# Transposed layernorm tiles of one chunk tracked in separate buffers instead of one

## The chip, the cores and the metric

One core of a Trainium2 chip. The metric is device time in microseconds (us) of one execution. "The granted clock" is the share of TensorE's full clock that the records show, as a mean over the run, rounded: 1.000 leaves room for about 1.2 us at half clock, 0.999 for 1.2 to 3.5 us (worked out from the rounding and a span of 1164 us).

## The reference, cut to what matters

The program is one transformer block with adaptive layernorm: 2048 tokens, width 1024, 32 query heads on 4 key/value heads with 512 cached positions, then a SwiGLU network of width 3584.

```python
h = _layernorm(x) * (1 + ca) + sa
x = x + ga * _A_ref(h, A_k_cache, A_v_cache, A_wq, A_wo)     # attention, output projection
h = _layernorm(x) * (1 + cb) + sb
x = x + gb * _B_ref(h, B_w_gate, B_w_up, B_w_down)           # gate, up, down
```

`h` is the moving operand of matmuls. The kernel keeps it for them as `hT`, with its width on the partitions, so it transposes the normalized tile.

## The kernel before

The tokens are worked on in chunks of 512 (four tiles of 128). Seven of the eight chunk layernorms of the program are made as follows (the very first one goes through TensorE). VectorE normalizes a tile into one of two buffers `nsc`, SyncE issues a DMA transpose of it into a quarter of the columns of `hT`, and when all four are there, VectorE scales and shifts each 128-row slice of `hT` (the modulation).

Every wait is made by a small tracker: an operation waits for the last writer of what it reads, and for the last writer and all readers of what it writes.

```python
def norm(t, sl, ns, c0=0, n=D, half=False):
    o = (nscf if half else nsc4)[ns]
    T.op(DVE, lambda: V.tensor_scalar(o[:, c0:c0 + n], x_res[:, t, c0:c0 + n], mv[sl][:, 0:1], rstd[sl],
                                      op0=ALU.subtract, op1=ALU.mult),
         reads=[B_x[t], B_mv[sl], B_rs[sl]], writes=[B_ns4[ns]])

def norm_turn(ch, tt, sl=None):
    t = ch * TPC + tt
    sl = t % 2 if sl is None else sl
    norm(t, t % 8, sl, half=True)
    T.op(Q_ln[sl], lambda: SP.dma_start_transpose(hT[ch % 2][:, :, tt * P:(tt + 1) * P], nscf[sl]),
         reads=[B_ns4[sl]], writes=B_hT[ch % 2])        # the same eight buffers for all four tiles
```

The four transposes write different columns, but they name the same buffers as written, so the tracker makes each wait for the landing of the one ahead. The wait stands in SyncE's queue, in front of what SyncE issues later: the next of attention's transposes was issued at 53.62 us in the trace of the kernel before, behind the fourth of these (51.40).

Chunk 1 is made inside the first heads of attention. There `pre0(i)` is the work ahead of head step `i`; weights for the later output projection are loaded by GpSimd in units of 512 KB (`unit_load`), the first two at step 8:

```python
NORMS = {3: (2,), 4: (0,), 5: (3, 1)}                    # step: tiles of chunk 1 normalized there

def pre0(i):
    ...                                                  # cut
    if i in (7, 8):
        load_wga(i - 7)
    ...                                                  # cut
    if i in (8, 9):
        for dt in range(4 * (i - 8), 4 * (i - 8) + 4):
            modulate(hT[1], B_hT[1], dt, 0, 0, B_mode)
    if i < NQ0 + 1:
        if i % 2 == 0:
            qproj(NQ0 - 1 + i // 2)                      # 8 matmuls, then VectorE evicts
    elif i + 3 < NDI:
        qproj(i + 3)
    for n, tt in enumerate(NORMS.get(i, ())):
        norm_turn(1, tt, (i + n) % 2)

def tick0(i):
    if 1 <= i < 5:
        next(x1_stats[0])                                # statistics of chunk 1, partly on GpSimd
    ...                                                  # cut
    if i == 8:
        chain[0] = unit_chain(0, HP)                     # its first step issues two unit_load
    if 8 <= i < NI - 8:
        unit_tick(i)
```

GpSimd waits for nothing at step 8, so these two loads go out as soon as the statistics are done (in the trace of the kernel before the last operation of these starts at 43.82 us, and the loads are issued at 44.33 and 45.27).

The softmax here doesn't subtract the row's maximum and nothing guards it: scores larger than these inputs give would overflow.

## Time and profile before

The first three runs had a median of 1165.69 us (1161.40 to 1168.27). The profiled one took 1166.38 us by the timer and 1164.5 us from first to last instruction; its clock was 0.997.

| Quantity | Value | View |
|---|---|---|
| TensorE busy | 1146.3 us of 1164.5 | page |
| VectorE busy | 817.9 us | page |
| SyncE's wait for landings of these transposes | 73.2 us, 21 times | waits of SyncE's queue |
| VectorE's wait for a free `nsc` | 31.0 us, 11 times | waits |
| TensorE's stall at chunk 1 | 2.9 us | waits, 36 to 64 us |

Lines of the page of the kernel before: the span, TensorE's row (busy us, share, instructions; the other engines follow), and the chain that ended last by engine.

```profile
span 1164.5 us, 18183 instructions
...
PE 1146.3 (98%) x7019; PEld 589.2 (51%) x7105; DVE 817.9 (70%) x1638; ACT 532.8 (46%) x745; POOL 68.4 (6%) x137
...
PE 93%; DVE 2%; DMA 2%; ACT 1%; issue 1%; POOL 0%; ACTq 0%; POOLq 0%; DVEq 0%
```

TensorE is busy in 98% of the span and makes 93% of the chain, so I look for the waits with which TensorE stands still. The waits of SyncE's queue in the kernel before (waiter <- waited for: us in total, times, longest):

```profile
SPq L80 <- DMA arena<-nsc: 73.2, 21, 8.5
```

This is the wait that the change takes away: `nsc` is the source of the transposes, `arena` holds `hT`. The waits between 36 and 64 us, in the kernel before:

```profile
DVE arena L432 <- DMA arena<-nsc: 3.0, 1, 3.0
PE ps L272 <- DVE arena L648: 2.9, 1, 2.9
PE ps L272 <- ACT arena L797: 1.1, 3, 0.5
DVE nsc L427 <- DMA arena<-nsc: 1.0, 1, 1.0
```

Line 432 is the modulation, 648 the eviction of a query projection that stands behind four modulations in VectorE's queue (they start at 55.07 us, it at 56.36). The timeline of the kernel before, 36 to 60 us (start, us, engine, line, operation, count, and in brackets the idle time before it and what ended that):

```profile
37.72 1.30 SPq L447 DMA_TRANSPOSE arena<-nsc  x1
...
41.20 1.23 SPq L447 DMA_TRANSPOSE arena<-nsc  x1
...
44.33 1.69 POOL L937 DMA_DIRECT2D arena<-in_A_wo_dram  x2
44.50 9.07 SPq L447 DMA_TRANSPOSE arena<-nsc  x2
...
53.62 2.58 SPq L822 DMA_TRANSPOSE arena<-arena  x2
55.07 1.38 DVE L432 TENSOR_SCALAR arena<-arena,gain,mod_bf 128x512 f16<-128x512 f16 x4 [3.03 <-DMA arena<-nsc]
...
57.10 3.17 PE L272 MATMUL ps<-arena 128*128 128x512 f16 x7 [2.90 <-DVE arena L648]
```

The entry of 9.07 us is the third and the fourth transpose: issued at 44.50 and at 51.40, the second only when the first had landed (51.34). The fourth landed at 55.04. Note the last line too: seven matmuls take 3.17 us, about twice their usual 0.216 us each. The stretch table (length, busy us and count of each engine, granted clock, share of the DMA engines, GB/s) says why:

```profile
36.00:54.00 18.00, 16.79 (x169) 10.83 (x170) 13.03 (x31) 16.64 (x27) 5.54 (x10) 1.00 0.72 133
54.00:64.00 10.00, 6.88 (x34) 3.40 (x33) 4.99 (x14) 3.07 (x3) 0.00 (x0) 0.66 0.84 237
```

The clock in the second stretch is 0.66; the clock record has 0.50 from 56.2 to 63.1 us. The same table for the stages under which the other six chunks are made (first and second output projection, first down projection):

```profile
250.00:358.00 108.00, 107.74 (x531) 50.07 (x535) 71.17 (x108) 16.54 (x25) 1.45 (x2) 1.00 0.63 159
550.00:655.00 105.00, 104.60 (x528) 49.35 (x533) 67.48 (x103) 14.31 (x21) 0.79 (x2) 1.00 0.60 162
819.00:912.00 93.00, 92.60 (x426) 41.88 (x429) 63.15 (x101) 11.22 (x19) 0.00 (x0) 1.00 0.61 179
```

TensorE idles there by 0.3 to 0.4 us in each.

### The profile page before, as it was taken

The numbers are of one execution on the slowest core, as the hardware profiler recorded it, in microseconds if no ns is written. First come the engines' busy times: TensorE is split into PE (matmuls) and PEld (weight loads), VectorE is DVE, ScalarE is ACT, GpSimd is POOL, SyncE is SP. The second block draws the span as 40 slices with busy tenths as digits, with TensorE's granted clock in tenths as the row PEclk, the third lists the DMA queues.
The fourth block names the chain that finished last, engine by engine and source line by source line (L and its number), as shares of the span: only waits on it lengthen the run. The fifth ranks groups of instructions, "written<-read, shape, count | busy, mean of one in ns | idle before, by whom it ended". The sixth has DMA issues, their size and how long they took to land.

```text
span 1164.5 us, 18183 instructions
## 1 busy us (share of the span) xinstructions
PE 1146.3 (98%) x7019; PEld 589.2 (51%) x7105; DVE 817.9 (70%) x1638; ACT 532.8 (46%) x745; POOL 68.4 (6%) x137
## 2 busy tenths in 40 slices
PE   9899999999999999999999999999999999999999
PEld 5565555654445666656544444444444444444444
DVE  4757997748476677776566798777557777776536
ACT  3856777740107777787110345454110344544110
POOL 1200221000001111111000001000000000000000
PEclk9999999999999999999999999999999999999999
DMA  9679799977916998844766232333765423234443
GB/s 323 137 194 220 197 226 201 207 155 192 268 34 158 192 205 198 202 112 105 191 181 199 73 107 74 83 99 100 203 178 166 122 73 109 73 90 131 133 160 110
DMA packets 289941, 179.98 MB, mean 155 GB/s; under 512 B 130496, under 2 KB 278080, under 8 KB 289856
## 3 DMA queue, kind: packets, MB, share of 16 engines
q1 hardware_dynamic: 226880, 92.31, 35.9%
q10 hardware_dynamic: 54336, 55.05, 14.9%
q0 software_dynamic: 8640, 31.46, 9.1%
q8 instruction: 56, 0.92, 0.3%
q14 instruction: 29, 0.24, 0.1%
HBM read 128.45 MB, written 19.92 MB: 127 GB/s over the span
## 4 chain that ended last, share of the span: by engine, by line
PE 93%; DVE 2%; DMA 2%; ACT 1%; issue 1%; POOL 0%; ACTq 0%; POOLq 0%; DVEq 0%
PE ps L272 93%; ACT arena L797 1%; DMA wo_sum<-arena 1%; DMA arena<-in_A_wo_dram 1%; DVE arena L827 1%; DVE arena L898 0%; DMA arena<-nsc 0%; PE ps L276 0%; DVE arena L819 0%; DVE st L413 0%; ACT arena L610 0%; DVE arena L595 0%; DVE arena L844 0%; DVE arena L948 0%; ACT tmp L735 0%
## 5 line engine op out<-in xcount | busy, mean ns | idle before, releaser
L272 PE MATMUL ps<-arena 128*128 128x512 f16 (+2 forms) x6714 | 1138.8, 330 | 15.4 <-DVE arena L648 2.9
L272 PEld LDWEIGHTS ps<-arena 128*128 128x128 bf16 (+1 forms) x6800 | 579.0, 98 | 568.3 <-issue 6.4
L797 ACT ACTIVATE arena<-ps 128x1024 bf16<-128x1024 f32 x256 | 261.4, 1022 | 50.1 <-PE ps L272 38.1
L830 ACT ACTIVATE tmp<-ps 128x512 f32<-128x512 f32 x167 | 99.7, 597 | 297.3 <-PE ps L272 274.3
L898 DVE TENSOR_TENSOR arena<-arena 128x512 f16<-128x512 bf16 x328 | 133.5, 420 | 3.0
L827 DVE TENSOR_TENSOR arena<-ps,tmp 128x512 bf16<-128x512 f32 (+1 forms) x134 | 91.9, 686 | 49.1 <-PE ps L272 37.8
L830 ACT ACTIVATE nsc<-ps 128x512 f32<-128x512 f32 x84 | 50.1, 596 | 93.1 <-PE ps L272 90.9
L819 DVE TENSOR_TENSOR arena<-ps,rl 128x512 f16<-128x512 f32 x128 | 88.5, 692 | 4.5
L827 DVE TENSOR_TENSOR arena<-ps,nsc 128x512 f16<-128x512 f32 x84 | 57.4, 687 | 41.2 <-PE ps L272 29.9
L816 DVE RECIPROCAL rl<-ps 128x4 f32<-128x4 f32 x128 | 23.3, 182 | 89.2 <-PE ps L272 88.2
L1539 ACT ACTIVATE arena<-arena 128x512 f16<-128x512 f16 x84 | 49.9, 625 | 32.4 <-DVE arena L827 32.4
L1036 DVE TENSOR_TENSOR arena<-arena 128x2048 f16<-128x2048 f16 (+3 forms) x56 | 56.2, 1013 | 9.3 <-PE ps L272 8.8
L1112 DVE TENSOR_TENSOR tmp<-ps,tmp 128x512 f32<-128x512 f32 x32 | 22.1, 690 | 50.3 <-ACT tmp L830 40.7
L830 ACT ACTIVATE arena<-ps 128x512 f32<-128x512 f32 x16 | 9.6, 597 | 89.3 <-PE ps L272 89.3
L948 DVE TENSOR_TENSOR arena<-arena 128x512 f16<-128x512 bf16 x120 | 47.9, 420 | 3.1 <-DMA arena<-in_A_wo_dram 2.0
L413 DVE BATCH_NORM_STATS2 st<-x_res 128x6 f32<-128x512 bf16 x58 | 39.6, 683 | 4.0 <-DMA x_res<-in_A_x_dram 3.8
L427 DVE TENSOR_SCALAR nsc<-x_res,mv,rstd 128x1024 f16<-128x1024 bf16 (+1 forms) x30 | 16.2, 541 | 31.0 <-DMA arena<-nsc 31.0
L1554 DVE TENSOR_TENSOR arena<-arena 128x512 f16<-128x512 f16 x84 | 35.0, 417 | 0.3
L1113 DVE TENSOR_TENSOR tmp<-tmp,rowb 128x512 f32<-128x512 f32 (+1 forms) x49 | 33.7, 687 | 1.7
L595 DVE SCALAR_TENSOR_TENSOR arena<-arena 128x1024 bf16<-128x1024 bf16 x24 | 29.2, 1216 | 0.0
L432 DVE TENSOR_SCALAR arena<-arena,gain,mod_bf 128x512 f16<-128x512 f16 x56 | 20.3, 409 | 4.4 <-DMA arena<-nsc 4.4
L1114 DVE TENSOR_TENSOR arena<-tmp,x_res 128x512 bf16<-128x512 f32 (+1 forms) x33 | 22.3, 676 | 1.1
(87 smaller groups left out, 332.8 us busy)
## 6 DMA issues: line engine op xcount, KB each, us to landing
arena<-in_A_wq_dram SPq DMA_DIRECT2D x28, 512.0 KB, 4.9
arena<-wo_sum ACTq DMA_DIRECT2D x7, 2048.0 KB, 9.2
arena<-in_B_w_gate_dram SPq DMA_DIRECT2D x28, 512.0 KB, 4.0
arena<-in_B_w_up_dram SPq DMA_DIRECT2D x28, 512.0 KB, 4.9
arena<-wd_sum ACTq DMA_DIRECT2D x8, 1792.0 KB, 8.0
arena<-in_B_w_down_dram ACTq DMA_DIRECT2D x6, 1792.0 KB, 7.2
arena<-in_A_wo_dram POOLq DMA_DIRECT2D x16, 512.0 KB, 4.9
wo_sum<-arena POOLq DMA_DIRECT2D x16, 512.0 KB, 4.4
```

Source lines behind the costliest of these rows:

```text
L272: T.op(PE, lambda: TE.matmul(out_ap, lhsT, rhs, start=start, stop=stop, skip_group_check=skip), reads=reads, writes=[bank_buf])
L413: T.op(DVE, lambda: V.bn_stats(st_[sl][:, hf * 6:hf * 6 + 6], x_res[:, t, hf * 512:hf * 512 + 512]), reads=[B_x[t]], writes=[B_st[sl]])
L797: T.op(ACT, lambda: A.activation(ex_s[es][:, 2 * kp:2 * kp + 2, :], banks2(SCB + 2 * kp), AF.Exp, scale=att_scale), writes=[PB[SCB + 2 * k ...
L819: T.op(DVE, lambda: V.tensor_tensor(o_s[os_].rearrange("p (a b) d -> p a b d", a=2), psap(PVB * 512, [[512, 2], [130, 2], [1, P]]), rlb, A ...
L827: T.op(DVE, lambda: V.tensor_tensor(out, bank(ba), other, ADD), reads=[ob2], writes=[PB[ba], ob])
L830: T.op(ACT, lambda: A.activation(dst, bank(bk), AF.Copy), writes=[PB[bk], db])
L898: T.op(st, lambda: eng.tensor_tensor(o, a, b, op), reads=rd, writes=[wr])
L948: T.op(DVE, lambda: V.tensor_tensor(o, a, b, SUB), reads=rd, writes=[wr])
L1036: T.op(DVE, lambda: V.tensor_tensor(o, a, b, SUB), reads=rd, writes=[sb])
L1113: T.op(DVE, lambda: V.tensor_tensor(tm, tm, rw, MULT), reads=[B_row[row]], writes=[tb])
L1539: T.op(ACT, lambda: A.activation(o, s_, AF.Silu), reads=[sb], writes=[ob])
L1554: T.op(DVE, lambda: V.tensor_tensor(gu[blk][:, p, :], o, s_, MULT), reads=[sb, ob], writes=[B_gu[blk][p]])
```

## The change

Each transpose gets a buffer of its own in the tracker, so it waits only for its source, and SyncE issues it without the landing of the one ahead (the fourth at 44.59 us in the trace of the changed kernel, where the third landed at 46.45). The modulation reads all four.

```diff
-            def modulate(dst, bufs, dt, gi, ccol, cbuf):
+            def modulate(dst, bufs, dt, gi, ccol, cbuf, tiles):
                 ...
-                     reads=[B_g[gi], cbuf, bufs[dt]], writes=[bufs[dt]])
+                     reads=[B_g[gi], cbuf] + tiles, writes=[bufs[dt]])
 
+            def ln_tiles(ch):
+                tiles = [_Buf("hTt%d_%d" % (ch, tt)) for tt in range(TPC)]
+                for tile in tiles:
+                    for b_ in B_hT[ch % 2]:
+                        tile.absorb(b_)
+                return tiles
 
-            def norm_turn(ch, tt, sl=None):
+            def norm_turn(ch, tt, tiles, sl=None):
                 ...
-                     reads=[B_ns4[sl]], writes=B_hT[ch % 2])
+                     reads=[B_ns4[sl]], writes=[tiles[tt]])
 
             def ln_task(ch, gi, ccol, cbuf):
+                tiles = ln_tiles(ch)
                 ...
+            x1_tiles = ln_tiles(1)          # chunk 1; its modulate and norm_turn calls get it
```

`absorb` takes over what the old buffers had to wait for, so the first write still waits for the readers of the chunk before.

More of the change, by code (lines that the diff above doesn't have):

```diff
@@ L447, in norm_turn @@
                 T.op(Q_ln[sl], lambda: SP.dma_start_transpose(hT[ch % 2][:, :, tt * P:(tt + 1) * P], nscf[sl]),
-                     reads=[B_ns4[sl]], writes=B_hT[ch % 2])
+                     reads=[B_ns4[sl]], writes=[tiles[tt]])
             def ln_task(ch, gi, ccol, cbuf):
                 dst, bufs = hT[ch % 2], B_hT[ch % 2]
+                tiles = ln_tiles(ch)
                 for tt in range(TPC):
-                    norm_turn(ch, tt)
+                    norm_turn(ch, tt, tiles)
                     yield
@@ L457, in ln_task @@
                 for dt in range(DT):
-                    modulate(dst, bufs, dt, gi, ccol, cbuf)
+                    modulate(dst, bufs, dt, gi, ccol, cbuf, tiles)
                     if dt % 2 == 1:
@@ L1250, in pre0 @@
                     for dt in range(4 * (i - 8), 4 * (i - 8) + 4):
-                        modulate(hT[1], B_hT[1], dt, 0, 0, B_mode)
+                        modulate(hT[1], B_hT[1], dt, 0, 0, B_mode, x1_tiles)
                 if i < NQ0 + 1:
@@ L1257, in pre0 @@
                 for n, tt in enumerate(NORMS.get(i, ())):
-                    norm_turn(1, tt, (i + n) % 2)
+                    norm_turn(1, tt, x1_tiles, (i + n) % 2)
                 if 1 <= i < 5:
```

## The prediction

> **What bounds the kernel.** TensorE: 1146.3 us busy of a 1164.5 us span (98%; page), and the chain of waits is 93% matmul. By the stretch table it idles 0.26 of 108 us in the first output projection (250 to 358 us), 0.4 of 105 in the second and 0.4 of 93 in the first down projection; but 4.5 us between 30 and 60 us.
>
> **What the change does.** No compute instruction is added or removed. SyncE's transposes of layernorm tiles wait 73.2 us (21 times, waits of its queue) for the landing of the one ahead; that goes. VectorE's normalization still waits for its source buffer (two alternate), so for the transpose two back. [...] in the trace before they already overlap attention's transposes, so I expect a correct result.
>
> **Six of the seven chunks** are made in the shadow of the projections. VectorE waits there 10.6, 12.5 and 6.8 us for landings (waits by stage), but TensorE does not stall. Those waits shrink and the time stays, within 0.5 us.
>
> **Chunk 1 is on the chain**, at 37 to 55 us, inside the first heads of attention. Timeline and landings: its transposes are issued at 37.7, 41.2, 44.5 and 51.4 us and land at 41.1, 44.4, 51.3 and 55.0. The third takes 6.8 us because two 512 KB weight loads of GpSimd, issued at 44.3 and 45.3 (landing at 51.1 and 52.8), share the DMA engines; the fourth, normalized by 45.1, is issued only when the third has landed. VectorE reaches the modulation at 52.04 and waits 3.03 us for the fourth. Behind four modulations stands the eviction that TensorE needs: it stalls 2.9 us (54.2 to 57.1). The clock record then shows 0.50 from 56.2 to 63.1: a 128x512 matmul starts every 0.43 us in place of 0.216, so the stall costs some 2.9 us a second time. [...]
>
> **After.** Transpose three is issued at about 43.8 and should land near 47. Transpose four is issued at about 45.2, shares the engines with the loads, and by my estimate lands at 49 to 52, against the modulation's turn at 52.04. The stall mostly goes, and with it the half clock: 2.9 + 2.9 = 5.8 us at most; I count 5.2. What follows is TensorE-bound, so it carries to the end.
>
> **Predicted: 1160.5 us**, range 1157.0 to 1165.5 (runs of before alone span 1161.4 to 1168.3). Faster by over 2%: 0.01; within 2%: 0.98; slower by over 2%: 0.01.
>
> **What would show it.** No TensorE wait above 1 us between 50 and 60 us, and PEclk 1.00 there; TensorE busy about 3 us less; the fourth transpose issued near 45 us; SyncE's wait for these landings far below 73 us; VectorE's 31.0 us wait for landings less than half; the projections' stretches unchanged.
>
> **What would make it wrong.** The fourth landing still after 53 us, because the weight loads or attention's transposes, now issued earlier too, hold it up: the stall and perhaps the half clock stay. Or the half clock comes from the many small gaps of 36 to 54 us: then only 2.9 us are gained. Or a queue freed earlier starts loads that collide elsewhere.

Of 2.9 us for the stall and 2.9 us for the half clock 5.2 us were counted, and 1165.69 less 5.2 is 1160.5. That the half clock comes from the stall was my assumption at this point; the trace shows a clock of 0.50 for 6.8 us, from 56.2 us on, 2.0 us into the gap of 54.2 to 57.1. The overlap that stands behind "I expect a correct result": in the trace of the kernel before, a layernorm transpose issued at 37.72 landed at 41.12, one of attention's issued at 39.06 landed at 41.69.

## The result

Six runs of the changed kernel: median 1162.68 us (1161.61 to 1165.12). Six of the kernel before: median 1165.44 us (1161.40 to 1168.27). The ratio is 0.9986, with a 95% interval of 0.9962 to 1.0010: the same within the noise. (Ratios here are the mean time of one kernel's runs over that of the other's of the same rounds, so not quite the ratio of the medians.) Executions over 1.5% slower than the fastest of the same kernel are left out of the means. All outputs are right. On a second chip, below, the same two kernels came out at 1.0009 (0.9990 to 1.0028).

The profiled runs are 1164.5 and 1159.8 us long. Page of the kernel after:

```profile
span 1159.8 us, 18164 instructions
...
PE 1143.1 (99%) x7019; PEld 588.2 (51%) x7105; DVE 817.5 (70%) x1638; ACT 532.5 (46%) x745; POOL 68.8 (6%) x137
```

Waits of the kernel after, 36 to 64 us:

```profile
DVE arena L432 <- DMA arena<-nsc: 2.1, 1, 2.1
PE ps L272 <- DVE arena L656: 2.0, 1, 2.0
PE ps L272 <- ACT arena L805: 1.1, 3, 0.5
```

Timeline of the kernel after, 36 to 60 us (its lines are 7 or 8 further down than those of before):

```profile
40.39 1.24 SPq L454 DMA_TRANSPOSE arena<-nsc  x1
...
43.23 2.70 SPq L454 DMA_TRANSPOSE arena<-nsc  x2
...
43.79 1.69 POOL L945 DMA_DIRECT2D arena<-in_A_wo_dram  x2
...
45.98 3.58 SPq L830 DMA_TRANSPOSE arena<-arena  x2
...
53.60 1.38 DVE L432 TENSOR_SCALAR arena<-arena,gain,mod_bf 128x512 f16<-128x512 f16 x4 [2.10 <-DMA arena<-nsc]
...
55.64 4.70 PE L272 MATMUL ps<-arena 128*128 128x512 f16 x29 [1.97 <-DVE arena L656]
```

Stretches of the kernel after:

```profile
36.00:54.00 18.00, 16.47 (x168) 10.70 (x168) 13.07 (x32) 16.61 (x27) 5.28 (x10) 1.00 0.87 151
54.00:64.00 10.00, 8.21 (x59) 4.48 (x61) 7.19 (x19) 4.37 (x5) 0.00 (x0) 1.00 0.81 255
...
250.00:358.00 108.00, 107.68 (x530) 50.08 (x535) 73.71 (x114) 19.92 (x29) 1.45 (x2) 1.00 0.56 152
550.00:655.00 105.00, 104.30 (x504) 48.24 (x508) 68.54 (x104) 12.80 (x19) 0.00 (x0) 1.00 0.64 173
819.00:912.00 93.00, 92.66 (x427) 41.79 (x430) 62.35 (x101) 10.91 (x19) 0.00 (x0) 1.00 0.63 176
```

The change did what it says: the third and fourth transpose of chunk 1 are now issued at 43.23 and 44.59 us, one right behind the other, and the 73.2 us line is gone from the waits of SyncE's queue. Much of that wait only changed its name, for SyncE now waits longer for VectorE in front of the same transposes. These two lines were 35.5 and 17.2 us in the kernel before (there L447, L1036 and L1052):

```profile
SPq L454 <- DVE arena L1044: 70.8, 14, 15.6
SPq L454 <- DVE arena L1060: 26.7, 4, 8.3
```

And the fourth transpose landed at 53.58, nine microseconds after its issue. TensorE still stalls 2.0 us. Attention's transposes behind it, 1.3 us each to issue before, took 1.7 to 2.8 us.

VectorE has the same 1638 records in the same order in both traces, so one can read where the 4.7 us arose. The same VectorE operation comes 0.5 us earlier just before the stall (48.26 against 47.73 us), 3.8 us earlier just after it (68.38 against 64.59), 4.8 us earlier at 186 us, and 4.7 us earlier at the end. So 0.5 us was there before chunk 1, 0.9 is the shorter stall, some 2.3 are the half clock, which this run of the changed kernel did not have, and 1.0 is a wait of VectorE for a unit load (2.0 us near 180 us) that stands in the first trace only. That fits the prediction almost too well. But two of the six runs of the changed kernel had a clock of 0.998, and those took 1164.4 and 1165.1 us. So the first question is whether the change made the difference at all, or whether two single profiles happened to fall that way.

### The profile page after: what moved, and what is told of

The parts are those of the page before. It is cut to its first block, busy times and chain, and to the rows that moved or that the text cites. A ratio compares the mean times of both kernels' runs of the same rounds, so it can differ in the third digit from the quotient of the medians.

```text
span 1159.8 us, 18164 instructions
## 1 busy us (share of the span) xinstructions
PE 1143.1 (99%) x7019; PEld 588.2 (51%) x7105; DVE 817.5 (70%) x1638; ACT 532.5 (46%) x745; POOL 68.8 (6%) x137
## 4 chain that ended last, share of the span: by engine, by line
PE 94%; DVE 2%; DMA 1%; ACT 1%; issue 1%; SPq 0%; POOL 0%; DVEq 0%; ACTq 0%
PE ps L272 94%; ACT arena L805 1%; DMA arena<-nsc 1%; DVE arena L835 1%; DMA arena<-in_w_mod_dram 0%; DVE arena L906 0%; PE ps L276 0%; DVE st L413 0%; SPq L310 0%; DVE arena L432 0%; SPq L341 0%; DVE arena L852 0%; ACT tmp L743 0%; DVE arena L1563 0%; ACT L1548 0%
## 5 line engine op out<-in xcount | busy, mean ns | idle before, releaser
L1044 DVE TENSOR_TENSOR arena<-arena 128x2048 f16<-128x2048 f16 (+3 forms) x56 | 56.2, 1013 | 9.3 <-PE ps L272 8.8
L427 DVE TENSOR_SCALAR nsc<-x_res,mv,rstd 128x1024 f16<-128x1024 bf16 (+1 forms) x30 | 16.2, 541 | 24.1 <-DMA arena<-nsc 23.4
L835 DVE TENSOR_TENSOR arena<-ps,rowb 128x512 f16<-128x512 f32 x28 | 19.3, 690 | 3.9 <-ACT rowb L838 3.4
```

The lines of the kernel that those rows point to most:

```text
L835: T.op(DVE, lambda: V.tensor_tensor(out, bank(ba), other, ADD), reads=[ob2], writes=[PB[ba], ob])
L1044: T.op(DVE, lambda: V.tensor_tensor(o, a, b, SUB), reads=rd, writes=[sb])
```

## The experiments

**Theory A** (the prediction's): the early issue makes the fourth transpose land early, and this removes the stall and the half clock. **Theory B**: the landing is set by the bytes that stand in front of the transpose in the DMA engines, above all the two 512 KB loads; the change only moves the wait from SyncE into the DMA queue. **Theory C**: the gain, if any, comes from the six chunks under the projections.

The landing times of chunk 1 are gathered here for all runs, from the transposes' issue records and semaphore events (us from the span's start):

| Run | Tiles of chunk 1 | 512 KB loads in the way | 3rd issued | 4th issued | 4th landed | Landed after issue of the 1st | TensorE's stall |
|---|---|---|---|---|---|---|---|
| before | one buffer | 2 | 44.50 | 51.40 | 55.04 | 17.3 | 2.9 |
| split_rest | one buffer | 2 | 44.88 | 50.24 | 54.05 | 15.9 | 1.7 |
| fill_before | one buffer | 2 | 44.72 | 51.92 | 55.38 | 17.3 | (filled) |
| after | apart | 2 | 43.23 | 44.59 | 53.58 | 16.3 | 2.0 |
| after_again | apart | 2 | 43.72 | 45.07 | 54.21 | 16.6 | 2.0 |
| split_x1 | apart | 2 | 43.45 | 44.81 | 55.11 | 17.6 | 3.2 |
| one_early | apart | 1 | 43.48 | 44.84 | 52.18 | 14.1 | 0.4 |
| early_wo | apart | 0 | 43.95 | 45.31 | 48.60 | 10.7 | none |
| early_wo_2 | apart | 0 | 43.40 | 44.75 | 48.04 | 10.6 | none |
| early_evac | apart | 0 | 43.76 | 45.11 | 48.44 | 10.8 | none |
| before_early_wo | one buffer | 0 | 45.53 | 48.66 | 51.75 | 14.2 | none |
| before_early_wo_2 | one buffer | 0 | 46.71 | 49.84 | 53.31 | 14.4 | none |
| before_early_evac | one buffer | 0 | 45.23 | 48.38 | 52.01 | 14.5 | none |

"None" means that VectorE did not wait for the landing, so TensorE did not either; waits of 0.3 to 0.9 us on other things remain. VectorE comes to the modulation 14.3 us after the first issue in the kernel before (52.04 less 37.72), so that is the landing that would be early enough.

### 1. The change for chunk 1 alone, and for the other six alone

```diff
# split_x1: the six chunks share one buffer again
-                tiles = ln_tiles(ch)
+                tiles = ln_tiles(ch)[0:1] * TPC
# split_rest: chunk 1 shares one buffer again
-            x1_tiles = ln_tiles(1)
+            x1_tiles = ln_tiles(1)[0:1] * TPC
```

> Only chunk 1 (built at 37 to 55 us) keeps its tiles apart; the six chunks built under the projections share one tracked buffer again, as before. My theory (all of the gain lies in chunk 1's stall at 54 to 57 us and the half clock after it): like the full change, profile span near 1160, stall at 54 to 57 us near 2.0 us instead of 2.9, mean ratio to before 0.997 to 1.000, and fewer runs with a clock below 0.999 than before has. Rival (the gain comes from VectorE's shorter waits for landings under the projections): same time as before, ratio 1.000.

> The opposite half: chunk 1 shares one tracked buffer as before, the other six chunks keep their tiles apart. My theory: same as before within 0.1%, the fourth transpose of chunk 1 again issued near 51 us, the TensorE stall of 2.9 us and the half clock back. Rival (projections): the whole gain of 1.7 us in the mean, ratio 0.9986.

Measured, on one chip: split_x1 1164.21 us median, ratio 1.0012 (0.9991 to 1.0033); split_rest 1162.85 us, 0.9997 (0.9979 to 1.0014); the kernel before 1162.85 us. Neither half gains. Waits of split_x1 between 36 and 64 us, and then its stretch table:

```profile
DVE arena L432 <- DMA arena<-nsc: 3.3, 1, 3.3
PE ps L272 <- DVE arena L656: 3.2, 1, 3.2
```

```profile
54.00:64.00 10.00, 6.51 (x34) 3.08 (x36) 5.95 (x15) 2.87 (x3) 0.00 (x0) 0.83 0.83 245
```

Waits of split_rest between 36 and 64 us, and then its stretch table:

```profile
DVE arena L432 <- DMA arena<-nsc: 1.8, 1, 1.8
PE ps L272 <- DVE arena L656: 1.7, 1, 1.7
```

```profile
54.00:64.00 10.00, 8.19 (x66) 4.54 (x64) 7.15 (x18) 4.58 (x6) 0.00 (x0) 1.00 0.90 265
```

Of my expectations only the time of split_rest held (within 0.1% of the kernel before); the ratio of split_x1, its clocks below 0.9995 (3 of 6 runs) and both stalls missed, and the stalls in opposite directions. The kernel with chunk 1's tiles apart had the longest stall of all (3.2 us) and a half clock (0.83 in the mean of 54 to 64 us; a span of 1164.1 us); the one without had the shortest of those with both loads (1.7 us), no half clock and a span of 1160.3. The stall varies from run to run by more than the change moves it. Theory A is in trouble, and theory C gets no support.

### 2. The changed kernel once more, on another chip

No edit.

> The change itself, unaltered, on this chip, for a second profile and a second ratio. So far the kernels with chunk 1's tiles apart landed its fourth transpose 16.3 and 17.6 us after the first was issued (the change, split_x1), those without 17.3, 15.9 and 17.3 (before, split_rest, fill_before). Theory now (the earlier issue only moves the wait from SyncE into the DMA queue, since the landing is set by the bytes in front of it): the fourth issued near 44.7, landed 16 to 17.6 us after the first's issue, stall 1.5 to 3.2 us, ratio 0.998 to 1.001. Rival (my prediction's): landed under 15 us after, no stall, ratio 0.996.

Measured: 1163.32 us median, ratio 1.0009 (0.9990 to 1.0028); the kernel before 1162.75 us. The fourth transpose was issued at 45.07 and landed at 54.21, a stall of 2.0 us. With both loads in the way, the landing comes on average 16.8 us after the first issue where the tiles share a buffer (17.3, 15.9, 17.3) and 16.8 us where they do not (16.3, 16.6, 17.6). The fourth transpose goes out 5 to 7 us earlier and lands no earlier (experiment 5 takes the landing times apart). This is what theory B says, and the prediction's rival number (under 15 us) is out.

### 3. The gap filled with matmuls of no use

```diff
+                if i == 9:
+                    for _ in range(13):
+                        mm(bank(XB), kT_sb[:, 0, :], kT_sb[:, 0:KT, :].rearrange("p a b -> p (a b)"), True, True, [B_kT[0]], PB[XB])
```

> The kernel before, with 13 matmuls of no use (128x512, 2.8 us) put on TensorE in the gap of 54.2 to 57.1 us. The landing and the resumption of work near 57.1 us stay as they are. My theory (the half clock of 56.2 to 63.1 us comes from that one gap): clock 1.000 in every run, time some 2.5 to 3 us below those runs of before that have clock 0.997, and equal to those that have 1.000. Rival (the half clock comes from the many small gaps between 36 and 54 us): half clock as often as before, time unchanged.

Measured: 1163.66 us median (1162.29 to 1164.52), ratio 1.0002 (0.9986 to 1.0018), clock 1.000 in all six runs. Waits and stretch of fill_before, 36 to 64 us:

```profile
DVE arena L432 <- DMA arena<-nsc: 3.1, 1, 3.1
```

```profile
54.00:64.00 10.00, 9.66 (x61) 4.68 (x60) 6.90 (x17) 3.40 (x5) 0.00 (x0) 1.00 0.79 225
```

VectorE waits as long as ever, TensorE is busy, and the clock stays at 1.00. The kernel before had a clock of 0.999 in 3 of 11 runs on this chip; those took 1165.6 us in the mean, the other eight 1162.6. These 3.0 us are not the half clock alone: a mean of 0.999 allows at most 3.5 us at half clock, which is worth 1.7 us. The rest would be a longer stall that goes with it, which no trace of these runs shows. And only about one run in four has it; none of the 33 later runs of the kernel before was as low as the 0.997 of the first profile. The filled kernel has no half clock and is still not faster: its mean is 1.0 us above those eight runs, which I expected it to equal. Perhaps the 2.8 us of matmuls overhang in runs whose stall is shorter (1.7 us in split_rest); that is not shown. Six runs alone would not settle that the gap is the cause; the count over all kernels, below, adds to it.

### 4. The two loads moved out of the way, without the change

```diff
                 if 1 <= i < 5:
                     next(x1_stats[0])
+                if i == 1:
+                    chain[0] = unit_chain(0, HP)
+                    next(chain[0])
                 ...
-                if i == 8:
-                    chain[0] = unit_chain(0, HP)
-                if 8 <= i < NI - 8:
+                if 9 <= i < NI - 8:
                     unit_tick(i)
```

GpSimd comes to the loads behind its first statistics operation of chunk 1 (33.48 us in the trace of this run).

> The kernel before, transposes still one behind the other's landing, but the two 512 KB weight loads of GpSimd that met chunk 1's third transpose are issued near 34 us instead of 44.3. My theory (serial landings cost time only because these loads stretch one landing to 6.8 us): the third transpose lands in about 3.5 us, the fourth is issued near 47.5 and lands near 51, TensorE's stall of 2.9 us goes wholly, clock 1.000, 3 to 5.5 us faster than a run of before with the half clock, as fast as the change or faster by 1 to 2 us. Rival (the serial chain of four landings is itself too long): the fourth still lands after 53 us and the stall stays over 1.5 us.

Measured: 1160.30 us median (1159.86 to 1160.53), ratio 0.9973 (0.9957 to 0.9990), clock 1.000 in all five fast runs. Timeline of before_early_wo, GpSimd from 30 to 46 us and SyncE from 33 to 60 us:

```profile
33.65 1.69 POOL L937 DMA_DIRECT2D arena<-in_A_wo_dram  x2
```

```profile
45.53 4.61 SPq L447 DMA_TRANSPOSE arena<-nsc  x2
50.19 2.57 SPq L822 DMA_TRANSPOSE arena<-arena  x2
```

The transposes still go one behind the other's landing, but the third now lands 3.1 us after its issue (48.59), and the fourth lands at 51.75, in time. TensorE's waits there, 36 to 64 us:

```profile
PE ps L272 <- DVE arena L819: 0.9, 1, 0.9
PE ps L272 <- DVE arena L432: 0.3, 1, 0.3
```

The serial order that the change removes costs TensorE at most these 0.3 us once the loads are gone. The traces also show where the gain is: the same VectorE operation comes 0.7 us later than in the first profile of the kernel before at 48.3 us, 5.4 us earlier at 68.4, and 6.2 us earlier at the end. So it arises at chunk 1, though that first profile is one of the slower runs.

### 5. The loads early and the change, and one load early

early_wo is the changed kernel with the same edit. one_early issues one load at step 1 and leaves the other at step 8:

```diff
+                if i == 1:
+                    chain[0] = unit_chain(0, HP)
+                    unit_load(HP)
                 ...
-                if i == 8:
-                    chain[0] = unit_chain(0, HP)
                 if 8 <= i < NI - 8:
                     unit_tick(i)
 # and the first step of unit_chain loads up to unit k0 + 1 only
```

> The change, and the two 512 KB loads issued near 34 us as in before_early_wo. Theory (with the loads out of the way the transposes land fast either way): clock 1.000, no stall of TensorE over 1 us at chunk 1, the fourth transpose landed near 48 us, time as before_early_wo (1160.3) within 0.5 us, since there its landing at 51.75 was already in time. Rival (the change pays once the loads are gone): 1 us or more below 1160.3.

> The change, with one of the two 512 KB loads issued near 34 us and the other left at 44. A dose between the change (two loads in the way) and early_wo (none). Theory (a transpose behind a load gets only about one 256-byte packet served for each 4096-byte packet of the load, so the landing shifts with the bytes of load in the way): the fourth transpose lands some 2 to 3 us later than in early_wo and 2 to 3 us earlier than in the change, near 50 to 51 us, stall under 0.5 us, time near 1160.5. Rival (the delay comes from something else that happens at that place, such as the 16 KB and 8 KB instruction fetches near 51 to 53 us): landing near 53 us as with both loads.

Measured: early_wo 1161.23 us median, ratio 0.9990 (0.9972 to 1.0008), one of six runs with clock 0.999; one_early 1160.73 us, 0.9984 (0.9966 to 1.0002), clock 1.000 in all; the kernel before 1162.75 us. early_wo missed its expected time (0.9 us above before_early_wo in the median, where 0.5 was expected, and on another chip). one_early landed at 52.18, between the 50 to 51 of the theory and the 53 of the rival. The waits of one_early, 36 to 64 us:

```profile
DVE arena L432 <- DMA arena<-nsc: 0.5, 1, 0.5
PE ps L272 <- DVE arena L656: 0.4, 1, 0.4
```

The dose is clear in the table of landings: 10.7 us after the first issue with no load in the way, 14.1 with one, 16.3 to 17.6 with two. The packet records show how. Counts in half a microsecond, from the trace of the changed kernel (the 4096-byte packets are the loads', the 256-byte packets the transposes'):

```
us            4096 B   256 B
44.5 to 45.0       0     395
45.0 to 45.5       0     401
...
47.0 to 47.5      36      15
47.5 to 48.0      40      28
48.0 to 48.5      38      49
48.5 to 49.0      36      43
49.0 to 49.5      43      43
...
51.0 to 51.5       0     535
```

In the five rows from 47.0 to 49.5 us the transposes fall from about 400 small packets in half a microsecond to 15 to 49, and get about one small packet for each large one: 178 against 193. In after_again it is 211 against 135 between 47.5 and 50.0 us. Equal shares by bytes would be sixteen small packets for a large one; the counts lie much nearer to one for one. How the DMA engines choose between the two was not shown. And the transpose that meets the loads is slow: the third in the kernel before (issued at 44.50, landed at 51.34), the fourth in the kernel after (44.59, 53.58).

The loads are not the whole delay in every profile. A landing shows as 16 steps of the transpose's semaphore, within 0.2 us in early_wo (48.40 to 48.60). In the trace of the changed kernel the fourth transpose's last packet ended at 51.45 (each transpose closes with 32 packets of 4 bytes, counted here in the order of issue); one step came at 51.94, the other fifteen only at 53.39 to 53.58. The same stop of some 1.4 us parts the steps in split_x1 (ten to 53.57, six from 55.04) and in one_early (two to 50.62, the others from 52.01). It is absent in after_again, where the loads themselves ended later (last packet at 53.07, not 50.73). Each stop begins 0.5 to 0.7 us after the first of two instruction fetches (16 KB and 8 KB) starts: at 51.3, 53.1 and 50.0 us. In early_wo these come at 49.2, after the landing. Whether the fetches make the stop was not tried, so the rival of one_early's expectation stands for this part.

As an estimate, with the stop taken off, the landings after the first issue are 10.7 us with no load, 12.7 with one, and 14.8, 16.6 and 16.1 with two. The dose keeps its order. But one_early then lands at 50.8, as its theory said, the changed kernel at about 52.1, and the three profiles with the tiles apart come to 15.8 in the mean against 16.8 with one buffer. So the early issue may win up to 1 us of landing, which these few profiles cannot settle.

### 6. The eviction ahead of the modulations

```diff
-                if i in (8, 9):
-                    for dt in range(4 * (i - 8), 4 * (i - 8) + 4):
+                if i == 9:
+                    for dt in range(4, 8):
                         modulate(...)
                 if i < NQ0 + 1:
                     if i % 2 == 0:
                         qproj(NQ0 - 1 + i // 2)
+                    if i == 8:
+                        for dt in range(0, 4):
+                            modulate(...)
```

With the early loads, on the changed kernel (early_evac) and on the kernel before (before_early_evac):

> As early_wo, and VectorE evicts the query projection that TensorE waits for ahead of the four modulations, not behind them. before_early_wo still showed waits of TensorE of 0.9 and 0.3 us there. Expected: those go, 0.3 to 1 us below early_wo: about 1159.5, the fastest of all. If it equals early_wo, nothing of the stall was left to take.

> before_early_wo with the eviction ahead of the four modulations, without the change: the smallest edit that I expect to be the fastest. TensorE's remaining waits at chunk 1 were 0.9 and 0.3 us in before_early_wo, so at most 1 us below it, clock 1.000 in all runs. If it equals before_early_wo, the order of the eviction is worth nothing there.

Measured: early_evac 1160.72 us median, ratio 0.9983 (0.9967 to 0.9999); before_early_evac 1160.56 us, 0.9977 (0.9955 to 0.9999). Neither is told apart from its neighbour without this edit, and early_evac is not the 1159.5 that I expected; one of six runs of before_early_evac had a clock of 0.999. TensorE's wait on the modulation grew from 0.3 to 0.6 us in before_early_evac while the one of 0.9 us fell to 0.3. The order is worth nothing that these runs can show.

### 7. The early loads with and without the change, on one chip

> before_early_wo once more, beside early_wo_2 on one chip, because the first comparison (1160.27 against 1161.77 in the mean) was made across two chips. Theory (the change buys nothing once the loads are early, and nothing is lost by it): the two means within 0.7 us, both 1.5 to 3 us below the kernel before. Rival (the change costs something elsewhere): early_wo_2 slower by over 1 us again.

> early_wo (the change and the early loads) once more, for the comparison said at before_early_wo_2: within 0.7 us of it in the mean by the theory, slower by over 1 us by the rival.

Measured: before_early_wo_2 1161.46 us median (1161.04 to 1169.52, seven runs), ratio 0.9982 (0.9959 to 1.0006); early_wo_2 1160.30 us (1159.87 to 1162.52), 0.9974 (0.9953 to 0.9996); the kernel before 1162.96 us. This time the changed one is ahead, by 1.2 us in the median (2.0 in the mean, 0.9 without the slowest run of the other); on two chips before it was behind by 0.9. The sign turns with the chip or the day, so "within 0.7 us" was too narrow, and the rival (the change costs something) is not borne out either.

The seventh run of before_early_wo_2, its profiled one, took 1169.52 us and shows another place: half clock for 3.4 us each at 11.9, 107.5 and 121.2 us, with two stalls of TensorE of 2.2 and 2.5 us between 96 and 126 us, where VectorE waited 3.2 us for an attention transpose and 3.3 us for a unit load. So not every half clock of a run comes from chunk 1.

Counted over all listed runs with a clock: kernels with both loads in the way and the gap not filled had a clock below 0.9995 in 18 of 57 runs (the kernel before 9 of 33, split_rest 1 of 6, the three with chunk 1 apart 8 of 18); kernels with the gap filled or with a load out of the way in 3 of 48. The change did not make it rarer.

## Why the prediction was right or wrong

The time, 1162.68 us, lies in the stated range, and "within 2%" was right. The reason given for the gain was not.

- *TensorE bounds the kernel, and the six chunks under the projections do not matter.* Right: their stretches are unchanged (0.3 to 0.7 us of idle before and after), and split_rest measures 0.9997.
- *SyncE's wait of 73 us goes, the third transpose is issued near 43.8 and lands near 47, the fourth is issued near 45.2.* Right: 43.23, 46.45 and 44.59.
- *The fourth "by my estimate lands at 49 to 52".* **This step failed.** It landed at 53.58, 54.21 and 55.11 in three profiles, no earlier than with the waits in place. The prediction had named the cause itself (it "shares the engines with the loads") and listed the outcome among what would make it wrong, but it gave no sum for the sharing and took too little for it. A transpose landed 3.3 us after its issue without the loads (early_wo), and 9.0 to 10.3 us after it beside them, getting about one 256-byte packet for each 4096-byte packet (178 to 193 in the trace of the changed kernel). In two of the three profiles some 1.45 us of this is the stop near the instruction fetches, which the prediction did not have at all and whose cause stays open (without it, as an estimate, the first of the three would have landed near 52.1, which is 53.58 less 1.45).
- *The stall "mostly goes": 2.9 us.* Failed with it. The stall was 2.0, 2.0 and 3.2 us with the tiles apart, 2.9 and 1.7 without.
- *"And with it the half clock": 2.9 us.* With the gap filled the clock was 1.000 in six of six runs. In the profiles a half clock came with gaps of 2.9 us (before) and 3.2 us (split_x1) at chunk 1, and a clock of 1.00 with gaps of 1.7 us (split_rest) and 2.0 us (after, after_again); how long a gap it takes was not shown. The size fits that one profile (some 2.3 us between the two traces), but it was counted in full. The kernel before has a clock below 0.9995 in 9 of 33 runs, and those on the chip of experiments 1, 3 and 4 took 3.0 us longer, stall included. So, as an estimate, the whole term was worth about 0.8 us in the mean (0.27 times 3.0), even if it had gone, and it did not go.
- *VectorE's 31.0 us wait for landings less than half.* Wrong: 23.4 us after, and 29.3 in split_x1, 24.0 in split_rest. A buffer comes free when its transpose lands, and in the median of all 28 that took 3.6 us from the issue before and 3.9 after.
- *5.2 us in all.* Measured: 1.7 us in the mean on the first chip (1164.76 less 1163.10), minus 1.0 on the second. The interval of both chips excludes the 0.9955 that was predicted (1160.5 over 1165.69). The 4.7 us between the two first profiles were mostly chance: the profile of split_rest, with chunk 1 as before, was 4.2 us shorter too.

What beats both kernels is the move of the two loads: 0.9973 and 0.9982 without the change, 0.9990 and 0.9974 with it. By these ratios it is 1.2 to 3.1 us, near the limit of what these runs resolve: two of the four intervals include 1.

## What to carry to other kernels

A wait taken out of an issuing queue need not be a gain: here the fourth transpose landed 16.8 us after the first was issued, in the mean, with the wait and without it. Ask whether the transfer then lands earlier and what is in the DMA engines with it, and count that in packets: here, next to a bulk load, 178 packets of 256 bytes went with 193 of 4096 bytes (the changed kernel) and 211 with 135 (after_again). Before removing an order of small transfers, look whether a bulk load that nobody needs yet can be moved: here this did what the change was meant to do (in before_early_wo the fourth transpose landed in time, at 51.75 us, and TensorE waited 0.3 us for the modulation). And where an effect comes in some runs only, one profile of each kernel can show the predicted difference by chance: repeat the profile, or run the half of the change that should show nothing.
